# Attention decode, one core: VectorE's program for 14 heads becomes a loop of two heads per pass

## The chip, the cores and the metric

The kernel runs on 1 core of one Trainium2 chip. The metric is device time in microseconds (us), as the median of several executions. An interval given with a ratio is a 95% interval. A ratio is the mean time of one kernel's fast runs over that of the other's fast runs of the same rounds, so it is not quite the ratio of the medians quoted.

## The reference

One query row per head attends to 8192 keys, for 16 heads of width 256, all in bf16:

```
B, H, Sq, Sk, D = 1, 16, 1, 8192, 256
scores = einsum("bhqd,bhkd->bhqk", q, k) * D ** -0.5
p = softmax(scores, axis=-1)
return einsum("bhqk,bhkd->bhqd", p, v)
```

K and V are 67.1 MB each, and every byte is used once, so the kernel has to move 134.2 MB.

## The kernel before

A key's scores come from a row product. Each of the 128 partitions holds 64 key rows of a head, in two loads ("halves") of 2 MB for K and two for V. Of each half's 32 rows, VectorE does 24 (multiply by the q row, sum, one score), and TensorE does 8. There are four buffers each for K and V. SyncE issues all loads from one queue, in the order K, V, K, V, with V about three loads behind K.

The engines' programs are lists of operations with named waits. TensorE's list already has a repeated body, emitted as a loop of two heads per pass. VectorE's list is written out for all 16 heads (shortened; P·V is the product of the softmax's weights with V):

```
def emit(self, e, eng, nc=None):
    ...
    loop = self.bodies if e == "pe" else []          # only TensorE loops
...
qb = sb([P, H * D], BF16, "qb")                      # q rows of all heads, on all partitions
S  = sb([P, H * J], FP32, "S")                       # scores of all heads, J = 64
...
for n, (h, x) in enumerate(kseq):                    # head h, half x
    for c in range(DVE_COLS):                        # 24 columns
        dve(tensor_tensor_reduce(prod[...], Kb[slot][:, c], qb[:, h],
                                 accum_out=S[:, h*J + x*HALF + c]))
        if x == 0 and h >= 1 and c == 9:  xmax(h - 1)   # global maximum g of the head before
        if x == 1 and h >= 1 and c == 9:  rcp(h - 1)
    if x == 1:  m = max over S of this head
...
for h in range(H - 1):                               # TensorE and ScalarE
    if h: softmax(h - 1)                             # transposes m, so that VectorE can form g
    k_turn(2*h); softmax2(h - 1); k_score(2*h); lmm(h - 1); pv(2*(h - 1))
    k_turn(2*h + 1); k_score(2*h + 1); pv(2*(h - 1) + 1); merge(h - 1); final(h - 1)
```

## Time and profile before

| | before |
|---|---|
| median of the first 3 runs | 341.18 us (339.85 to 341.74) |
| span in the profile | 337.9 us |
| VectorE busy | 280.7 us (83%) |
| DMA rate, 260 to 300 us | 427 GB/s, share 1.01 |
| instruction queues | 0.13 MB (17 packets) and 0.07 MB (4 packets) |

The page of the kernel before. A queue line gives packets, MB, and the packets' time as a share of 16 DMA engines' span. A group line gives line, engine, operation, operands, count, busy us, mean ns, then the idle time before the group.

```profile
span 337.9 us, 5534 instructions
...
q1 hardware_dynamic: 10080, 134.22, 93.9%
q14 instruction: 17, 0.13, 0.1%
q8 instruction: 4, 0.07, 0.1%
...
L348 DVE CUSTOM_DVE_ANT_0 prod<-Kb,qb 128x256 bf16<-128x256 bf16 x768 | 268.5, 411 | 2.4 <-DMA Kb<-in_k_dram 1.9
...
L319 DVE TENSOR_REDUCE g<-misc 1x1 f32<-1x128 f32 x16 | 4.5, 278 | 38.1 <-PE misc L518 38.1
```

The load is the bound: 134.2 MB at 427 GB/s is 314 us. VectorE has slack, 38.1 us of waiting for TensorE before g.

The view by stretches for the end of the run (start:end, length, busy us and instructions of PE, PEld, DVE, ACT and POOL, TensorE's granted clock as a share of full speed, DMA share, GB/s):

```profile
260.00:300.00 40.00, 28.43 (x198) 12.31 (x199) 36.30 (x211) 10.79 (x22) 0.00 (x0) 0.83 1.01 427
...
318.00:320.00 2.00, 2.00 (x8) 0.71 (x7) 1.97 (x13) 0.00 (x0) 0.00 (x0) 0.72 0.06 25
320.00:324.00 4.00, 1.64 (x10) 0.55 (x9) 3.50 (x22) 0.00 (x0) 0.00 (x0) 1.00 0.06 27
324.00:328.00 4.00, 4.00 (x24) 1.76 (x23) 0.37 (x2) 0.82 (x4) 0.00 (x0) 1.00 0.06 26
```

The chain of waits, last part (start us, us, what; here and below, pieces called issue, of up to 0.04 us, are left out):

```profile
273.89 29.89 DMA Vb<-in_v_dram
303.82 3.63 PE acc L577 x16
307.48 0.59 ACT ac L592
308.11 1.02 PE acc L599 x4
309.13 0.32 PE misc L518 x2
309.48 0.28 DVE g L319
...
323.25 0.23 DVE m L367
```

The V load of head 13, second half, is in full at 303.8 us. TensorE's list has its P·V first, and it starts 0.04 us after that, at 303.82 us (16 matmuls, 3.63 us); then come the merge and the transposed maxima of head 14, on which VectorE's g waits. From there VectorE does the rest of head 15 in 13.8 us. Call that load **V13b**.

### The profile page before, as it was taken

The page shows a single profiled execution, that of the slowest core. Times are in us where ns is not written, and L with a number is a line of the kernel's source. Part 1 is how long each engine was busy: PE and PEld are TensorE (multiplying, and loading weights), DVE is VectorE, ACT ScalarE, POOL GpSimd, SP SyncE. Part 2 cuts the span into 40 slices and gives each one's busy share as a digit, 9 for nine tenths or more (in the row PEclk, how much of TensorE's full clock was granted, in tenths as well). Part 3 has the DMA queues.
Part 4 walks back from the last instruction along what each step waited for, and adds up shares of the span by engine and source line. Part 5 has one row for each costly group of instructions (what it writes and reads, how often), then busy time and mean ns, then how long its engine had stood idle before and what let it go on. Part 6 is the DMA issues. An engine that isn't in the chain of part 4 may idle for free.

```text
span 337.9 us, 5534 instructions
## 1 busy us (share of the span) xinstructions
PE 249.6 (74%) x1742; PEld 113.7 (34%) x1742; DVE 280.7 (83%) x1619; ACT 95.7 (28%) x186; POOL 0.2 (0%) x4
## 2 busy tenths in 40 slices
PE   1756866887768868678886768868688767677977
PEld 0532333242333323233332333323333323333435
DVE  7799989499796978969799696987969998796930
ACT  2542242122423213242122422213232312324210
POOL 0000000000000000000000000000000000000000
PEclk9999998777898777898778987778987959789699
DMA  7999999999999999999999999999999999999500
GB/s 275 431 429 431 430 425 428 427 427 431 425 429 425 428 429 432 424 429 429 428 431 424 427 429 431 428 423 432 421 434 427 422 433 427 429 429 418 219 23 3
DMA packets 10137, 134.44 MB, mean 398 GB/s; under 512 B 1139, under 2 KB 1156, under 8 KB 1925
## 3 DMA queue, kind: packets, MB, share of 16 engines
q1 hardware_dynamic: 10080, 134.22, 93.9%
q14 instruction: 17, 0.13, 0.1%
q8 instruction: 4, 0.07, 0.1%
q10 hardware_dynamic: 36, 0.02, 0.0%
HBM read 134.23 MB, written 0.01 MB: 397 GB/s over the span
## 4 chain that ended last, share of the span: by engine, by line
DMA 62%; DVE 18%; PE 16%; ACT 1%; issue 1%; SPq 1%; DVEq 0%
DMA Vb<-in_v_dram 58%; DVE prod L348 16%; PE acc L577 13%; DMA Kb<-in_k_dram 4%; PE acc L599 2%; ACT ac L592 1%; SPq L306 1%; PE misc L518 1%; DVE S L348 1%; DVE g L319 1%; ACT o L621 0%; DVE m L367 0%; PE misc L528 0%; DVE w L329 0%; DVE recip L327 0%
## 5 line engine op out<-in xcount | busy, mean ns | idle before, releaser
L348 DVE CUSTOM_DVE_ANT_0 prod<-Kb,qb 128x256 bf16<-128x256 bf16 x768 | 268.5, 411 | 2.4 <-DMA Kb<-in_k_dram 1.9
L577 PE MATMUL acc<-Vb,E 128*2 128x512 bf16 (+1 forms) x544 | 159.6, 463 | 25.9 <-DMA Vb<-in_v_dram 25.9
L470 ACT ACTIVATE KT<-tp 128x1024 bf16<-128x1024 bf16 x64 | 62.0, 1021 | 111.8 <-PE tp L461 111.8
L577 PEld LDWEIGHTS acc<-Vb,E 128*2 128x2 bf16 (+1 forms) x544 | 52.3, 100 | 119.8 <-issue 71.8
L348 DVE DVE_READ_ACCUMULATOR2_ANT S<- 128x1 f32 x768 | 56.5, 74 | 0.0
L487 PE MATMUL spe<-qcur,KT 128*128 128x1 bf16 x512 | 22.6, 166 | 32.5 <-ACT KT L470 32.5
L461 PE MATMUL tp<-identb,Kb 128*128 128x128 bf16 x512 | 37.4, 232 | 5.0 <-DMA Kb<-in_k_dram 5.0
L461 PEld LDWEIGHTS tp<-identb,Kb 128*128 128x128 bf16 x512 | 31.6, 104 | 15.4 <-issue 14.9
L319 DVE TENSOR_REDUCE g<-misc 1x1 f32<-1x128 f32 x16 | 4.5, 278 | 38.1 <-PE misc L518 38.1
L592 ACT ACTIVATE ac<-acc 2x512 f32<-2x512 f32 x15 | 8.8, 586 | 83.7 <-PE acc L577 82.5
L487 PEld LDWEIGHTS spe<-qcur,KT 128*128 128x128 bf16 x512 | 17.1, 97 | 39.6 <-ACT KT L470 39.6
L599 PE MATMUL acc<-ac,w 2*1 2x256 f32 x60 | 15.3, 373 | 9.5 <-ACT ac L592 9.5
L599 PEld LDWEIGHTS acc<-ac,w 2*1 2x1 f32 x60 | 3.6, 77 | 20.9 <-ACT ac L592 16.8
L614 ACT ACTIVATE o<-acc 1x256 bf16<-1x256 f32 x15 | 5.6, 373 | 16.8 <-PE acc L599 16.8
L518 PE MATMUL misc<-ident,m 128*1 128x128 f32 x32 | 6.3, 278 | 5.0 <-DVE m L367 5.0
L528 PE MATMUL misc<-g,ones_row 1*128 1x1 f32 x32 | 6.3, 262 | 1.2 <-DVE g L319 1.2
L528 PEld LDWEIGHTS misc<-g,ones_row 1*128 1x128 f32 x32 | 4.9, 191 | 3.4 <-DVE g L319 1.5
L535 ACT ACTIVATE negb<-misc 128x1 f32<-128x1 f32 x16 | 2.9, 178 | 10.4 <-PE misc L528 10.4
L542 ACT ACTIVATE E<-S,negb 128x64 bf16<-128x64 f32 x16 | 5.6, 348 | 0.5
L408 ACT ACTIVATE qb<-tp 128x512 bf16<-128x512 f32 (+1 forms) x9 | 4.6, 548 | 3.2 <-PE tp L400 3.2
L518 PEld LDWEIGHTS misc<-ident,m 128*1 128x1 f32 x32 | 1.4, 80 | 12.1 <-issue 6.1
L327 DVE RECIPROCAL recip<-misc 2x1 f32<-2x1 f32 x16 | 2.4, 150 | 3.6 <-PE misc L557 3.6
(30 smaller groups left out, 31.9 us busy)
## 6 DMA issues: line engine op xcount, KB each, us to landing
Kb<-in_k_dram SPq DMA_DIRECT2D x31, 2048.0 KB, 23.7
Vb<-in_v_dram SPq DMA_DIRECT2D x31, 2048.0 KB, 28.6
Kb<-in_k_dram SPq DMA_DIRECT2D x1, 1024.0 KB, 7.5
Vb<-in_v_dram SPq DMA_DIRECT2D x1, 1024.0 KB, 19.3
Kb<-in_k_dram SPq DMA_DIRECT2D x2, 256.0 KB, 3.0
Kb<-in_k_dram SPq DMA_DIRECT2D x1, 512.0 KB, 4.8
Vb<-in_v_dram SPq DMA_DIRECT2D x1, 512.0 KB, 20.2
Vb<-in_v_dram SPq DMA_DIRECT2D x2, 256.0 KB, 20.4
```

The source lines that it names most:

```text
L319: lambda e: e.tensor_reduce(g[0:1, s : s + 1], misc[s][0:1, MT0 : MT0 + P], AX.X, ALU.max),
L348: lambda e, slot=slot, c=c, col=col, h=h, r=(ttr - 1) % PROD: e.tensor_tensor_reduce(out=prod[:, r * D : (r + 1) * D], in0=Kb[slot][:, c * ...
L461: lambda e, c=c, hf=hf, i=(b * NH + hf) * P, view=view: e.transpose(view[:, i : i + P], Kb[slot][:, c * D + hf * P : c * D + (hf + 1) * P] ...
L470: lambda e, gn=gn, view=view: e.activation(out=KT[gn % KT_SLOTS][:, :], in_=view[:, 0 : GROUP * D], func=ACT.Copy),
L487: lambda e, b=b, hf=hf, oc=oc, gn=gn: e.matmul(spe[sl(h)][:, oc : oc + 1], lhsT=KT[gn % KT_SLOTS][:, (b * NH + hf) * P : (b * NH + hf + 1) ...
L518: lambda e: e.matmul(misc[s][0:1, MT0 : MT0 + P], lhsT=m[:, s : s + 1], rhs=ident[:, :], start=True, stop=True),
L528: lambda e: e.matmul(misc[s][:, BC0 : BC0 + 1], lhsT=ones_row[0:1, :], rhs=g[0:1, s : s + 1], start=True, stop=True),
L542: lambda e: e.activation(out=E[:, s * J : (s + 1) * J], in_=S[:, h * J : (h + 1) * J], func=ACT.Exp, bias=negb[:, h : h + 1], scale=SCALE, ...
L577: lambda e, c=c, col=col: e.matmul(a[0:step, 0 : step * D], lhsT=E[:, col : col + step], rhs=Vb[slot][:, c * D : (c + step) * D], start=(x ...
L592: lambda e: e.activation(out=ac[s][:, :], in_=acc[s][0:2, :], func=ACT.Copy),
L599: lambda e, i=i: e.matmul(acc[s][0:1, 0:D], lhsT=w2[0:2, 2 * s + i : 2 * s + i + 1], rhs=ac[s][0:2, i * D : (i + 1) * D], start=(i == 0), ...
L614: lambda e: e.activation(out=o[0:1, h * D : (h + 1) * D], in_=acc[s][0:1, 0:D], func=ACT.Copy),
```

## The change

The intent is a shorter VectorE program: heads 1 to 14 become seven passes of one body of two heads. For that, addresses must repeat every two heads. So the score buffer shrinks to two heads, and the q row is read from a two-place buffer `qbc`, which ScalarE fills for each later head.

```
-        loop = self.bodies if e == "pe" else []
+        loop = self.bodies[e]
...
-        qb = sb([P, H * D], BF16, "qb")
+        qb = sb([P, (H - 2) * D], BF16, "qb")
-        S = sb([P, H * J], FP32, "S")
+        S = sb([P, 2 * J], FP32, "S")
+        qbc = sb([P, 2 * D], BF16, "qbc")
...
+            if h and x == 0 and (h - 1) % UNROLL == 0:
+                plan.mark("dve")
             for c in range(DVE_COLS):
-                col = h * J + x * HALF + c
+                col = sl(h) * J + x * HALF + c
...
-                        in1=qb[:, h * D : (h + 1) * D],
+                        in1=qbc[:, sl(h) * D : (sl(h) + 1) * D],
...
+        def q_row(h):
+            s = sl(h)
+            act(lambda e: e.activation(out=qbc[:, s*D:(s+1)*D], in_=qb[:, (h-2)*D:(h-1)*D], func=ACT.Copy),
+                f"qbc{h}", [f"qb{h}", f"kfree{2 * prev(h) + 1}"], ksem("qbc", h))
...
                 lmm(h - 1)
+                if h + 1 < H:
+                    q_row(h + 1)
                 pv(2 * (h - 1))
```

(Cut: semaphores per head parity, the two-place reciprocals, and the bookkeeping of marks per engine.) The kernel also sets the place of the loop head (`head_slot` 0).

## The prediction

> **What bounds the kernel.** The load of K and V. The DMA part of the page gives 134.2 MB; the stretches view shows 427 to 428 GB/s and a DMA share of 1.00 to 1.01 in every 40 us stretch from 20 to 300 us. That is about 313 us of the 337.9 us span. The rest is 2.6 us until the first load is issued and about 19 us after the last V byte (near 318 us), in which VectorE ends head 15 (its maximum at 323.25 us) and TensorE does the last softmax and P·V.

> VectorE is busy 280.7 us (83%). In the timeline one score column starts every 0.345 us; a head takes about 17.5 us, and the DMA needs about 19.6 us for it. The difference shows in the list of waits: 38.1 us in 15 waits of the global maximum (g) for TensorE, most of them 2.1 to 3.1 us. No VectorE idle time is put down to "issue", so instruction fetch costs it nothing visible now.

> **What the change does.**
> - Removes fetched program: the instruction queues moved 0.13 + 0.07 MB. About 0.08 MB less is 0.2 us at 428 GB/s (estimate).
> - Adds a back edge per pass: some 18 register additions for wait values (my count) and a compare-and-branch.[...] No run yet shows these.[...]
> - Refetch: [...] no refetch. No run yet shows a VectorE loop.
> - Adds 14 ScalarE copies of a q row, about 0.3 us each (estimate from the 0.35 us exponential), on an engine 28% busy. They stand after the exponential, before evictions whose transposes come 5 us later; the row they overwrite was done with a head earlier. No wait for qbc expected.
> - The two-place score buffer orders nothing new: the exponential of head h-1 precedes the q row copy of head h+1 on ScalarE.

> **Critical part.** None in the steady stage. A pass ends just ahead of nine columns and the wait for g, so about 2 us of loop cost only shortens that wait. A late free slot costs nothing at once: loads land 24 to 29 us after issue but move in 4.9 us, so five or six are queued. The tail starts from the g of head 14, with 2.6 us of VectorE waiting before it; only more than that reaches the end.

> **Prediction.** 341.0 us, 80% range 339.0 to 343.0. Faster by over 2%: 0.02; within 2%: 0.94; slower by over 2%: 0.04.

> **What would show it.** DMA stays at 1.00 and 427 to 428 GB/s; VectorE busy stays 280 us; instruction bytes fall to about 0.12 MB; gaps under 1.5 us at pass boundaries, with the g waits shorter by as much on every second head (38 us to about 30); a ScalarE group of 14 copies and no VectorE wait on it; last maximum within 1 us of 323.

> **What would make it wrong.** A refetch through the saturated DMA of over 4 to 5 us at each back edge would use up VectorE's 2 us per head and make VectorE the bound: 345 to 360 us. A stall at loop exit above 2.6 us would lengthen the tail one for one. A gain over 2% would need instruction fetch to be stealing DMA time that I cannot see.

The forecast's sum came to 341.0 us, in line with the 341.18 us of the kernel before less 0.2 us of fetched bytes.

## More of the kernel before

After 318 us the DMA does not stop: for 10 us it moves 25 to 27 GB/s at a share of 0.06. One sixteenth of 427 GB/s is 26.7, and one sixteenth is 0.0625. One DMA engine of the 16 is still loading while the other 15 have finished.

## The result, and the profile after

The changed kernel took 331.19 us (median of 4, 330.99 to 331.35), beside 341.46 us for the kernel before (median of 4). The ratio is 0.9707, interval 0.9675 to 0.974: 3% faster. The prediction said 341.0, with a 2% chance of a gain of over 2%.

The page after:

```profile
span 329.4 us, 5609 instructions
...
q1 hardware_dynamic: 10080, 134.22, 96.3%
q8 instruction: 4, 0.07, 0.1%
q14 instruction: 7, 0.06, 0.0%
...
L358 DVE CUSTOM_DVE_ANT_0 prod<-Kb,qbc 128x256 bf16<-128x256 bf16 x768 | 268.7, 411 | 9.2 <-issue 5.9
...
L327 DVE TENSOR_REDUCE g<-misc 1x1 f32<-1x128 f32 x16 | 4.4, 278 | 22.6 <-PE misc L544 22.6
...
L436 ACT ACTIVATE qbc<-qb 128x256 bf16<-128x256 bf16 x14 | 5.6, 400 | 0.0
```

VectorE's columns are as long as before (411 ns). Its loop costs 5.9 us of "issue" in 8 gaps, and the wait for g absorbs them. That wait fell by more, from 38.1 us to 22.6; in e5 below, with the same gaps but a late load again, it is 28.2 us, so part of the fall goes with the earlier loads. Queue 14 has 7 packets in place of 17.

The stretches after:

```profile
260.00:300.00 40.00, 30.94 (x221) 13.58 (x220) 35.16 (x202) 12.34 (x24) 0.00 (x0) 0.87 1.01 428
...
318.00:320.00 2.00, 2.00 (x16) 1.02 (x14) 0.37 (x2) 0.66 (x2) 0.00 (x0) 1.00 0.13 50
320.00:324.00 4.00, 4.00 (x34) 2.55 (x33) 0.00 (x0) 0.37 (x1) 0.00 (x0) 1.00 0.01 4
```

The rate in the steady stage has not changed (428 GB/s against 427), but the 10 us of one engine's traffic are gone.

The chain of waits after:

```profile
268.95 26.28 DMA Vb<-in_v_dram
295.27 3.63 PE acc L605 x16
298.93 0.59 ACT ac L620
299.57 1.02 PE acc L627 x4
300.58 0.32 PE misc L544 x2
300.93 0.28 DVE g L327
...
314.70 0.23 DVE m L377
```

It is the same chain, 8.5 us earlier: V13b is in at 295.3 us in place of 303.8. The two spans differ by the same 8.5 us.

**Where the 8.5 us were.** The trace also records every semaphore increment of a load: 16 for each of the loads, and the core has 16 DMA engines. It does not name the engine of an increment. I read each as one engine's part that has landed, and the trace of the kernel before fits: the last V load has its 15th increment at 318.54 us and its sixteenth at 329.31, and from 318 to 328 us a sixteenth of the rate moves (25 to 27 GB/s); the P·V starts 0.04 us after V13b's sixteenth increment (303.82 and 303.78 us). Sorted by time, V13b's increments read (us after the span's start; worked out from the trace's records, no view prints them):

```
                first engine   15th engine   last engine   last minus 15th
before             291.80         293.93        303.78          9.85
after              292.05         294.53        295.23          0.70
```

The first engine is equally early in both. Fifteen engines agree within 2.5 us. In the kernel before, one engine is 9.85 us late, and the load waits for it.

That engine did not start late. In the kernel before, its distance to the 15th is 0.06 us at 54 us, then 0.96, 2.00, 2.94, 3.94, 4.96, 5.9, 6.9, 7.9, 8.9 and 9.85 us: ten steps, each just after one 8 KB packet of queue 14 (at 58, 85, 112, 136, 162, 186, 214, 238, 263 and 288 us). The packets around one of them, on that DMA engine (start us + ns, queue, bytes; chained by matching each packet's end to the next one's start):

```
135.571+619 q1 16384 | 136.187+324 q14 8192 | 136.498+1273 q1 16384 | 137.768+612 q1 16384
```

The instruction packet takes the engine for 311 ns, and the data packet after it takes 1273 ns in place of about 613. Together that is 0.97 us (why the data packet takes longer, no run shows). The engine does not make this up: between two steps the distance stays within 0.1 us.

The same mark, a data packet of 1265 to 1273 ns right after, is on eleven packets of queue 14 before V13b lands: these ten and one at 34 us, which met an engine that was still ahead of the others. In the changed kernel it is on two, at 29 and 48 us. Nine packets fewer at 0.97 us are 8.7 us, and V13b lands 8.55 us earlier. The other four packets (14, 92, 239 and 294 us) are followed by data packets of 988 to 1166 ns and leave no step; whose instructions they hold is not shown.

### The profile page after: what moved, and what is told of

Same layout as the page of the kernel before. It is cut to its first block, busy times and chain, and to the rows that moved or that the text cites. A ratio compares the mean times of both kernels' runs of the same rounds, so it can differ in the third digit from the quotient of the medians.

```text
span 329.4 us, 5609 instructions
## 1 busy us (share of the span) xinstructions
PE 243.8 (74%) x1742; PEld 112.2 (34%) x1742; DVE 281.4 (85%) x1619; ACT 100.0 (30%) x200; POOL 0.2 (0%) x4
## 4 chain that ended last, share of the span: by engine, by line
DMA 54%; DVE 27%; PE 14%; issue 2%; ACT 1%; SPq 1%; DVEq 0%
DMA Vb<-in_v_dram 50%; DVE prod L358 25%; PE acc L605 11%; DMA Kb<-in_k_dram 4%; PE acc L627 2%; SPq L314 1%; ACT ac L620 1%; DVE S L358 1%; PE misc L544 1%; DVE g L327 1%; DVE w L337 0%; DVEq L138 0%; ACT o L649 0%; DVE m L377 0%; PE misc L555 0%
## 5 line engine op out<-in xcount | busy, mean ns | idle before, releaser
L358 DVE CUSTOM_DVE_ANT_0 prod<-Kb,qbc 128x256 bf16<-128x256 bf16 x768 | 268.7, 411 | 9.2 <-issue 5.9
L605 PE MATMUL acc<-Vb,E 128*2 128x512 bf16 (+1 forms) x544 | 153.9, 450 | 20.6 <-DMA Vb<-in_v_dram 20.6
L605 PEld LDWEIGHTS acc<-Vb,E 128*2 128x2 bf16 (+1 forms) x544 | 51.0, 97 | 110.2 <-issue 66.3
L516 PE MATMUL spe<-qcur,KT 128*128 128x1 bf16 x512 | 22.6, 165 | 32.1 <-ACT KT L499 32.1
L327 DVE TENSOR_REDUCE g<-misc 1x1 f32<-1x128 f32 x16 | 4.4, 278 | 22.6 <-PE misc L544 22.6
L436 ACT ACTIVATE qbc<-qb 128x256 bf16<-128x256 bf16 x14 | 5.6, 400 | 0.0
```

The costliest lines, as they stand in the source:

```text
L327: lambda e: e.tensor_reduce(g[0:1, s : s + 1], misc[s][0:1, MT0 : MT0 + P], AX.X, ALU.max),
L358: lambda e, slot=slot, c=c, col=col, h=h, r=(ttr - 1) % PROD: e.tensor_tensor_reduce(out=prod[:, r * D : (r + 1) * D], in0=Kb[slot][:, c * ...
L436: lambda e: e.activation(out=qbc[:, s * D : (s + 1) * D], in_=qb[:, (h - 2) * D : (h - 1) * D], func=ACT.Copy),
L516: lambda e, b=b, hf=hf, oc=oc, gn=gn: e.matmul(spe[sl(h)][:, oc : oc + 1], lhsT=KT[gn % KT_SLOTS][:, (b * NH + hf) * P : (b * NH + hf + 1) ...
L605: lambda e, c=c, col=col: e.matmul(a[0:step, 0 : step * D], lhsT=E[:, col : col + step], rhs=Vb[slot][:, c * D : (c + step) * D], start=(x ...
```

## The experiments

The landing of V13b in each run, and the span of the same profiled run (us):

```
run                     first    15th     last   last-15th   span   span-last
before                 291.80   293.93   303.78    9.85     337.9    34.1
changed                292.05   294.53   295.23    0.70     329.4    34.2
e1_unrolled            292.32   295.15   304.64    9.49     340.5    35.9
e2_three_passes        291.82   294.15   300.71    6.56     334.8    34.1
e3_pool_1536           292.37   294.53   295.58    1.05     329.7    34.1
e4_before_pool_1536    292.01   294.32   303.88    9.56     341.4    37.5
e5_pool_memsets        292.32   295.10   300.62    5.52     334.8    34.2
e6_before_pool_memsets 292.42   300.91   304.54    3.63     340.4    35.9
e7_pe_unrolled         292.08   295.58   295.84    0.26     330.0    34.2
e8_four_heads          292.63   294.00   308.20   14.20     344.5    36.3
e9_one_engine          294.57   298.26   307.78    9.52     345.2    37.4
e10_all_engines        295.63   297.88   299.00    1.12     334.8    35.8
e11_early_max          291.73   294.39   295.14    0.75     326.9    31.8
e12_changed_again      292.28   295.17   295.72    0.55     331.5    35.8
e13_early_max_again    292.25   294.26   295.25    0.99     327.9    32.7
```

Read it by columns. Leaving out the two runs with added loads, the first engine stays within 1 us whatever the program. The last engine moves by 13 us. The tail after it is 34 to 37.5 us, but for the two runs that change the tail on purpose.

### e1_unrolled: the loop undone, all the rest kept

```
-        loop = self.bodies[e]
+        loop = self.bodies[e] if e == "pe" else []
```

> The changed kernel with VectorE's program written out again; the two-place q row and score buffers, the ScalarE copies and the semaphores stay. Theory F (instruction fetch: VectorE's 8 KB instruction packets all go through one of the 16 DMA engines, each puts that engine about 1 us behind, and every load waits for its last engine): queue 14 moves 0.13 MB in 17 packets again, the last engine of the V loads is 10 to 11 us behind the next one at the end, time 340 to 342 us. Theory B (the buffers and the changed ScalarE order brought the gain): time stays at 331 us.

Measured: 340.87 us (339.9 to 342.33), ratio to the kernel before 0.9997 (0.995 to 1.0043). One engine is 9.49 us late, and queue 14 is nearly back at its 17 packets:

```profile
q14 instruction: 16, 0.13, 0.1%
```

B falls: the buffers, the 14 copies and the semaphores together are worth nothing that these runs can tell from noise (0.5%). The gain comes with the loop.

### e2_three_passes: a loop over heads 1 to 6 only

```
-            if h and x == 0 and (h - 1) % UNROLL == 0:
+            if h and x == 0 and (h - 1) % UNROLL == 0 and h <= 7:
```

> The changed kernel with a loop of three passes (heads 1 to 6) and heads 7 to 15 written out. Theory F: about 8 heads of 107 instructions, 55 KB, 6 to 7 packets more than in the changed kernel, at 0.97 us each: 337 to 338 us, the lag of one engine growing only after head 6. Theory L (the loop itself runs VectorE faster, for instance by hidden fetch stalls of VectorE): gain in proportion to the looped heads, 3 of 7 passes, 337 us too, but with no lag of one engine. Theory B: 331 us.

(Its 55 KB, like the KB of the expectations below, are 64 bytes an instruction; see e8 for the numbers.)

Measured: 337.86 us (336.72 to 340.26), ratio 0.9941 (0.9887 to 0.9995). The late engine stays 0.76 us behind the 15th up to 124 us, and the distance then grows with each packet: 1.74 us at 154 us, 3.69 at 215, 5.61 at 275. The time fits F and L alike; the growth after the loop ends is what F asked for, and L says nothing of it.

### e3_pool_1536 and e4_before_pool_1536: no-operations on GpSimd (failed as experiments)

```
+            @block.gpsimd
+            def _(e):
+                for _ in range(1536):
+                    e.nop()
```

> The changed kernel, VectorE looping, plus 1536 no-operations on GpSimd, which has no other work: 12 blocks of 8 KB to fetch[...]. Theory F: 8 to 12 more instruction packets, and if all go through one DMA engine about 1 us each: 339 to 343 us, although VectorE's program is untouched. Theory L and theory B: 331 us, for neither VectorE nor the buffers change.

> The kernel before plus the same 1536 no-operations on GpSimd. Theory F: if GpSimd's packets go through another DMA engine than VectorE's, the loads wait for the slower of two lagging engines and nothing is added: 341 to 343 us; if through the same engine, the lags add up: 349 to 353 us. A theory of stolen total bandwidth would add about 0.1 MB over 428 GB/s, 0.2 us.

Measured: 332.45 us (331.19 to 334.2) and 342.97 us (341.65 to 343.94), ratios 0.9773 (0.9716 to 0.9829) and 1.0063 (1.0012 to 1.0113). The compiler had dropped the no-operations: the profiles count 5609 and 5534 instructions, as without them, and the first run's instruction packets are those of the changed kernel. So these two are repeats of the changed kernel and of the kernel before, and they show how far equal programs can differ: 0.6%.

The table says where that comes from. In the run of e4 that was profiled, the tail was 37.5 us long in place of 34.1. Of that, 16 P·V matmuls after V13b took 5.32 us against 3.63, and a later group of 8 took 3.19 against 1.73, in stretches with a lower granted clock (0.76 from 303 to 310 us, 0.72 from 324 to 330 us; in the trace of the kernel before, 1.00 in both).

### e5_pool_memsets: something else to fetch, VectorE untouched

```
+        scratch = sb([1, 1536], FP32, "scratch")
...
+            @block.gpsimd
+            def _(e):
+                for i in range(1536):
+                    e.memset(scratch[0:1, i : i + 1], 0.0)
```

> The changed kernel plus 1536 memsets of one element each on GpSimd, on a scratch row that nothing reads (the no-operations tried earlier were dropped by the compiler). VectorE's program and buffers are untouched. Theory F: 8 to 12 more instruction packets of 8 KB in queue 14; if one DMA engine carries them all, about 0.97 us of lag each: 339 to 343 us. Theories L (the VectorE loop itself) and B (buffers): 331 us. If VectorE's column mean stays at 411 ns, the memsets did not slow VectorE.

Measured: 337.31 us (336.56 to 338.43), ratio 0.9923 (0.9888 to 0.9957). The page of this run:

```profile
q14 instruction: 19, 0.16, 0.1%
...
L359 DVE CUSTOM_DVE_ANT_0 prod<-Kb,qbc 128x256 bf16<-128x256 bf16 x768 | 268.7, 411 | 9.5 <-issue 5.9
...
L737 POOL MEMSET scratch<- 1x1 f32 x1536 | 51.2, 89 | 8.2 <-issue 7.9
```

Twelve packets more, the last at 61 us. From 75 us on one engine is 5.5 us late, and still is when V13b lands, 5.4 us later than in the changed kernel; the span is 5.4 us longer too. VectorE loops as in the changed kernel, at 411 ns a column, so L falls. So does the theory of total bytes: 0.1 MB is 0.2 us at 428 GB/s.

I had expected 339 to 343 us. The miss is one of size: a GpSimd packet costs its engine about 0.65 us (309 ns, and the data packet after it takes 960 ns in place of 613), not VectorE's 0.97. And the first three packets, up to 16 us, left no lag behind (0.04 us at 21 us); nine at 0.65 us make the 5.5 us measured, within 0.4.

### e6_before_pool_memsets: two late engines

The same memsets in the kernel before.

> The kernel before plus the same 1536 memsets on GpSimd. Theory F with GpSimd's packets on another DMA engine than VectorE's: two engines lag by about 10 us each, the loads wait for the later one, so 341 to 344 us, nearly nothing added. Theory F with one engine for both: lag of about 20 us, 349 to 353 us.

Measured: 341.07 us (339.82 to 343.8), ratio 1.0026 (0.9962 to 1.009). The same twelve fetches that cost 5.4 us of landing time in the changed kernel cost 0.8 here (V13b at 304.54 in place of 303.78). The landings show two late engines: at the load landing at 320 us, the 14th engine is 2.99 us after the first, the 15th 8.49 us, and the last 13.06 us. GpSimd's packets take another engine than VectorE's, and a load waits for the later one. A cost of fetching that simply adds up per packet does not survive this run; the lag of the slowest engine does.

### e7_pe_unrolled: TensorE's loop written out

```
-        loop = self.bodies[e]
+        loop = self.bodies[e] if e == "dve" else []
```

> The changed kernel with TensorE's program written out in place of its loop; VectorE keeps its loop. About 2600 instructions more to fetch, 167 KB, 10 packets of 16 KB in queue 8. Theory F: 10 to 20 us of lag of one DMA engine (0.97 us per 8 KB at most doubles for 16 KB), 341 to 351 us. Theories L and B: 331 us, as VectorE and the buffers do not change.

Measured: 333.51 us (331.95 to 334.8), ratio 0.9813 (0.978 to 0.9845). The queues of this run:

```profile
q8 instruction: 13, 0.21, 0.3%
q14 instruction: 7, 0.06, 0.0%
```

My expectation of 10 to 20 us was wrong. There are nine packets more, of 16 KB each, twice the bytes that VectorE's unrolled program adds, and V13b's last engine moves by 0.6 us only. By the working above, a packet of 1.02 to 1.11 us with a data packet of 1.08 to 1.16 us after it puts its engine about 1.5 us behind (estimate); nine on one engine would be 13 to 14 us. Late in the run (the load landing at 311 us) six engines stand 3.2 to 4.2 us after the first, where in the changed kernel one does beyond 3.1. The delays are there, but over several engines. So TensorE's fetches are not all served by one engine, and F has to be put more narrowly: what costs here is not fetching (0.6 us with nine packets over several engines), but fetching again and again through the same DMA engine (9.85 us of lag with ten).

### e8_four_heads: a loop body twice as long

```
-            if h and x == 0 and (h - 1) % UNROLL == 0:
+            if h and x == 0 and (h - 1) % 4 == 0:
```

> The changed kernel with a VectorE loop of four heads per pass (3 passes, heads 1 to 12; 13 to 15 written out), a body of about 425 instructions, 27 KB. Theory F, and the body stays in the instruction memory: about 3 packets more than in the changed kernel, 333 to 335 us. Theory F, and the body no longer stays: some 3 to 4 packets again in each of two more passes, 339 to 342 us, with instruction packets of queue 14 all through the run.

Measured: 346.33 us (343.69 to 347.41), ratio 1.0162 (1.0106 to 1.0218). This is a loop, and slower than no loop. VectorE's waits and the queues of this run:

```profile
DVE prod L358 <- issue: 15.6, 4, 6.3
```

```profile
q14 instruction: 20, 0.16, 0.1%
q8 instruction: 4, 0.07, 0.1%
```

Counted between two loop branches in the trace, a pass of this kernel has 418 instructions, or 26.8 KB at 64 bytes each (estimate: in the kernel before, VectorE runs 1148 instructions from the first to the last of the ten packets, 128 to each of nine packets of 8 KB, and in e5 1536 memsets added twelve packets). A pass of the changed kernel has 210, or 13.4 KB. The longer body is fetched again in each pass: packets of queue 14 come all through the run, VectorE waits at the back edge (the branch from the end of a pass to its start) for up to 6.3 us, and one engine ends 14.2 us late. My expectation for this branch was 339 to 342 us; it fetches even more than I had counted, as much as the unrolled program and more.

### e9_one_engine and e10_all_engines: a late engine without any instructions

```
+            if kind == "v" and 2 <= n < 18:
+                plan.op("sp", lambda e, i=n - 2: e.dma_start(
+                    extra[:, i*512 : (i+1)*512],
+                    k[0, i].rearrange("(p j) d -> p (j d)", p=P)[0:17, 0:512]),
+                    f"x{n - 2}", dma=(s_x, 16 * (n - 1)))
```

(e10: 16 rows of 544 elements.) That 17 rows go to one engine, and 16 rows to all, was my assumption before the runs. The traces show 288 packets more in queue 1 with 17 rows (18 per load), 512 with 16 rows (32 per load); at V13b the last engine is 9.52 us behind the 15th with 17 rows, 1.12 us with 16.

> The changed kernel plus 16 small loads from HBM into a scratch tile that nothing reads, one after each of 16 V loads in the first half, each of 17 rows of 1 KB: [...] one DMA engine should carry it alone. 0.28 MB in all, no instruction fetched. Theory F as a theory of one late engine: about 0.65 us of data[...] each, 10 to 17 us of lag of one engine, 340 to 348 us. A theory in which instruction fetch acts otherwise (stalled sequencers, total bandwidth): 0.28 MB over 428 GB/s is 0.7 us, so 331 to 333 us.

> The control for the run with 17 rows: the same 16 small loads, the same bytes, as 16 rows of 1,088 bytes, which all 16 DMA engines share. Theory F: 0.04 us per engine and load, under 1 us of lag, 331 to 333 us. A theory of total bytes or of the number of loads: the same time as with 17 rows.

(The first: its 0.65 us is 17 KB at a sixteenth of 428 GB/s, 10.4 us for 16 loads, the lower end of its 10 to 17; 9.52 us of lag were measured. The 0.04 us of the second is 1,088 bytes at the same rate.)

Measured: 346.34 us (345.41 to 348.04), ratio 1.0175 (1.0129 to 1.0221), and 336.68 us (336.61 to 337.76), ratio 0.9901 (0.9866 to 0.9937). The stretches of the run with 17 rows show the same signature as the kernel before, 26 to 27 GB/s to the end:

```profile
324.00:328.00 4.00, 3.08 (x11) 0.84 (x8) 4.00 (x24) 0.00 (x0) 0.00 (x0) 0.79 0.06 27
328.00:332.00 4.00, 2.79 (x8) 0.97 (x9) 1.41 (x8) 0.00 (x0) 0.00 (x0) 0.64 0.06 26
```

The changed kernel itself took 331.2 to 332.9 us in its three sets of runs. Over that, the same 0.28 MB, 0.2% of the traffic, costs 13 to 15 us on one engine and 4 to 5.5 us on sixteen. So one late engine suffices, with no instruction fetched for it.

The control missed its expectation of 331 to 333 us. Its first engine lands V13b at 295.63 us, 3.6 us later than in the changed kernel, so the small loads held up all engines by about 0.22 us each; the rate from 60 to 220 us fell from 428 to between 418 and 422 GB/s. With 17 rows, too, the first engine is 2.5 us later, although, with one engine late, the other 15 should have had nothing more to do. Why is left open.

### e11_early_max, then e12_changed_again and e13_early_max_again: a shorter tail

The other half of the chain is the tail. TensorE's transpose of the maxima stands behind the P·V that waits for V13b, and need not:

```
-            if h:
-                softmax(h - 1)
             k_turn(2 * h)
...
             k_score(2 * h + 1)
             if h:
+                softmax(h)
                 pv(2 * (h - 1) + 1)
```

(plus `softmax(0)` ahead of the loop, and the one after the loop left out.)

> A try at a faster version: the changed kernel with TensorE's transpose of the row maxima of head h issued before the second half of P V of head h-1, so that VectorE's global maximum does not wait behind the late V load. Theory F: the load stays the bound in the steady stage, the wait of g goes from 22 us to under 10 us, and in the tail the last maximum of head 15 comes up to 2 us earlier: 329 to 331 us. If the tail is bound by the landing of the last V load instead: 331 us.

> The changed kernel once more, on one chip with its variant that issues the transpose of the maxima early. Theory F: 331 to 332 us, last engine of the V load of head 13 at 295 to 296 us, and from there 34 us to the end, or up to 36 where TensorE's granted clock is halved just then.

> The early transpose again, now beside the changed kernel on the same chip. If the tail of 34 us after the landing of the V load of head 13 is the other half of the chain, this shortens it by about 2 us with the landing unmoved at 295 us: 329 to 330 us, 0.5 to 0.7 per cent under the changed kernel. If the early transpose only gained by chance of the chip, both are alike.

(A halved granted clock is in the traces: 0.50 from 320 to 324 us in e8 and in e9.)

Measured: 329.68 us (328.67 to 330.04), ratio 0.9688 (0.9659 to 0.9716). Then on one chip, 5 rounds: the changed kernel 332.94 us (331.0 to 333.72), ratio 0.9765 (0.9724 to 0.9806), and this variant 329.70 us (328.82 to 330.79), ratio 0.968 (0.9641 to 0.972). The two ranges do not touch; the variant is about 0.9% under the changed kernel (0.968 over 0.9765) and beats both kernels.

V13b lands where it did (295.1 to 295.7 us in all three runs), and the tail is 31.8 and 32.7 us in place of 34.2 and 35.8. The end was not held by the last V byte, the other theory of the expectation: in e11 it lands at 320.7 us, as in the changed kernel (320.8), but the last 56 matmuls start at 318.6 us in place of 321.1. The chain of the variant's second run, and of the changed kernel beside it:

```profile
299.54 0.19 DVE g L327
...
313.22 0.23 DVE m L377
313.50 0.38 PE misc L544 x2
313.87 1.73 PE acc L605 x8
```

```profile
301.42 0.28 DVE g L327
...
315.19 0.23 DVE m L377
315.46 0.54 PE misc L544 x2
316.00 3.25 PE acc L605 x8
```

g comes 1.9 us earlier, and the last maximum with it. The remaining difference is in the 8 matmuls, 1.73 us in one run and 3.25 in the other. In the first pair of profiles the changed kernel had 1.73 there too. That is the scatter of the tail within one program, and it fits with medians of the kernel before and the changed one that differ by more (10 us) than the two traces (8.5 us): the profiled run of the kernel before, 339.69 us, was faster than all its timed runs (339.85 to 341.87).

## Why the prediction was wrong

Point by point:

- *"The load of K and V" as the bound, 427 to 428 GB/s and a share of 1.00 to 1.01:* right, and unchanged after.
- *Instruction bytes fall to about 0.12 MB:* right (0.06 + 0.07).
- *Gaps under 1.5 us at pass boundaries, absorbed by the wait for g:* right in kind. The gaps at the back edge were 0.62 to 0.68 us, with one of 1.67 us on entering the loop and one of 0.40 us on leaving it; VectorE's eight branches took 50 to 69 ns, and the 18 register additions of my count had been merged into 3 instructions per pass. The waits for g fell to 22.6 us, not to about 30; e5 (28.2 us) points to the loads, which came earlier too.
- *"No refetch":* right for this body (210 instructions in the trace): from 50 to 305 us the last engine's distance to the 15th stays at 0.69 to 0.74 us, without a step. e8 shows that it was no idle worry: with a body of 418 queue 14 has 20 packets in place of 7, and the loop is worse than none (346.33 us).
- *14 ScalarE copies off the critical path:* right (400 ns each, expected 300; VectorE waited for `qbc` once, 0.2 us).
- *Last maximum within 1 us of 323:* wrong, 314.70.

The step that failed is *"About 0.08 MB less is 0.2 us at 428 GB/s (estimate)"*. The instruction bytes did fall (by 0.07 MB), but the step spread them over 16 DMA engines. VectorE's all pass one of them, at 0.97 us a packet: ten packets up to V13b are 9.7 us, and 9.85 us of lag were measured, 0.70 us after the change. V13b lands 8.55 us earlier, so the term was too small by a factor of over 40. This is not only a size: the mean share of the DMA engines was the wrong quantity, and the right one here is the lag of the slowest engine.

Two readings led there. I read *"the last V byte (near 318 us)"* from a rate that had fallen from 427 GB/s; it had fallen to 26, not to zero, and the last V bytes landed at 329.3 us. And I took *"no VectorE idle time is put down to issue, so instruction fetch costs it nothing"* as the end of the matter. It is true of VectorE's own instructions. The cost fell on the loads. The prediction did name the door, *"a gain over 2% would need instruction fetch to be stealing DMA time that I cannot see"*; it could be seen, in the last three stretches.

## What to carry to other kernels

In this kernel, bound by loads, a bulk load was over when its slowest DMA engine was: V13b's 15th engine was done at 293.93 us, its last at 303.78, and the P·V started at 303.82. What repeatedly visited one engine (a long straight program's instruction fetch, small loads of 17 rows) delayed the later loads, and its cost was its time on that engine (0.97 us for an 8 KB packet of VectorE), not its share of the bytes. Look at the end of the load stream: a rate that falls to a sixteenth (25 to 27 GB/s of 427) and stays there for some microseconds was one late engine here, with and without fetches. A loop cured it here only with a body that was not fetched again: one of 210 instructions on VectorE was not (331.19 us), one of 418 was (346.33 us). Where between the two the limit lies, no run shows.
